# Windowed attention with a gated MLP: all loads through one GpSimd queue, 64-column transposes, and a new list of steps

## The chip, the cores and the metric

One Trainium2 chip, one core. The metric is the device time of one execution in microseconds (us), as a median over several runs. Lower is better. The engines are named as in the profile: PE (TensorE, matrix multiplications), PEld (its weight loads), DVE (VectorE), ACT (ScalarE), POOL (GpSimd) and SP (SyncE, which here only issues transfers).

## What is computed

Four batches, eight heads, 768 positions, head size 64. First an attention with a sliding window of 128 and four sink positions that every query sees, then a block with a gated MLP whose gate mixes along the sequence:

```python
scores = scale * np.matmul(q, k.transpose(0, 1, 3, 2))
keep = (pos[None, :] < 4) | ((rel >= 0) & (rel < 128))        # rel = query position - key position
a = softmax(np.where(keep, scores, -1e9))
x = np.matmul(a, v)                                           # heads side by side: [4, 768, 512]
h = gelu_tanh(x @ w_in)                                       # [4, 768, 1024]
u, v = h[..., :512], h[..., 512:]
v_n = (v - mean(v)) / np.sqrt(var(v) + 1e-6) * g_ln
v_s = np.einsum('ts,bsd->btd', w_sg, v_n) + b_sg[None, :, None]
out = x + (u * v_s) @ w_out
```

All inputs and the output are float32; the kernel multiplies in bf16.

## The kernel before

Everything that the kernel does is cut into small steps, each a function of a few instructions. The string STEPS (lines 15 to 64) lists some 700 of them, and the loop at line 500 issues them in that order. Each engine executes its own instructions strictly in that order, so the list alone decides which work stands ahead of which; a step whose input is late holds up all later steps of its engine. Numbers behind a name are the batch, then the pair of heads (four pairs a batch), then a part. HOLDS (line 68) adds two orders by hand: the loads LQ.1.0 and LG wait until the transfer LWS has landed.

The steps, in the order in which a batch passes through them:

- LQ, LK, LV (lines 171 to 179) load q, k and v of one pair of heads as float32 through SP's queue. q and k come with six consecutive positions of a head in each partition, v with single positions of 64 values. LW, LWS and LWO (lines 196 to 205) load the three weight matrices through GpSimd's queue, which turns float32 into bf16 on the way. LC (line 207) fetches the v of the sink positions through ACT's queue.
- CQ, CK, CV (lines 185 to 194) cast them to bf16, all on GpSimd (line 182).
- TQ, TK (lines 269 to 272, helper at 261) transpose a pair on PE: six transposes of 128 columns, where the two heads of the pair stand side by side. EQ (line 274, DVE) and EK (line 279, ACT) copy the result out of PSUM.
- QK (line 303) multiplies, with one head in the upper and one in the lower 64 rows of the array; EX (line 315, ACT) takes the exponential; MK (line 320) masks, on DVE by a product (line 325) or on GpSimd by two selections (lines 329 and 333). KS, SK, SX (lines 283 to 301) do the same for the sink positions. Batch 0 does this for each pair, the later batches once for all four pairs. SK of a later batch is four products of 512 columns that are added up in one tile.
- AV (line 340) multiplies by v, NR (line 365, DVE) divides by the sums.
- XT, XE (batch 0, PE and ACT) or XD (a transposing transfer) turn the result. MV and MU (lines 394 and 442) multiply by w_in, GV and GU (ACT) apply the gelu.
- BN (line 406, DVE) takes mean and variance, RS (line 414, GpSimd) the inverse root, Z (line 430, DVE or ACT) normalizes. WT and WE turn w_sg once.
- SP (line 463, PE) mixes along the sequence, GT (line 470, DVE) adds the bias, GM (line 475, DVE) multiplies by u, OU (line 479, PE) multiplies by w_out, RA (line 486, DVE) adds x, ST (line 489) stores.

The attention of batch b+1 is mixed with the MLP of batch b. Tiles are handed out from rings (line 110); the two rings in PSUM have 2 and 4 tiles.

Of the kernel before, what the change touches and what calls it, by code (L numbers as in the profile page):

```python
# [15 lines left out]
IDEN ZERO LC MASK LQ.0.0 LK.0.0 LQ.0.1 LK.0.1 VSK LQ.0.2 LK.0.2 LV.0.0 LQ.0.3 LK.0.3 CQ.0.0 LV.0.1 LV.0.2 TQ.0.0  # L16
CK.0.0 VSM.1 LV.0.3 EQ.0.0 TK.0.0 CQ.0.1 EK.0.0 VSM.3 TQ.0.1 CK.0.1 VSM.0 QK.0.0.2 QK.0.0.1 EX.0.0.2 KS.0.0 TK.0.1
EQ.0.1 CQ.0.2 SK.0.0 VSM.2 TQ.0.2 CK.0.2 EQ.0.2 SX.0.0 QK.0.0.0 MK.0.0.2 TK.0.2 EX.0.0.1 CV.0.0 EK.0.2 MK.0.0.1
EX.0.0.0 QK.0.2.2 KS.0.2 CQ.0.3 EX.0.2.2 MK.0.0.0 QK.0.2.0 LW.0 EK.0.1 QK.0.2.1 LW.1 EX.0.2.1 AV.0.0.0 KS.0.1 TQ.0.3
# [4 lines left out]
AV.0.3.0 NR.0.3.0 XT.0.3 XE.0.3 MV.0.2 MU.0.3 GV.0.2 LQ.1.0 LK.1.0 WT.3 WT.4 LV.1.0 WE.3 WT.5 LG WT.2 WE.4 GU.0.3
MV.0.0 WE.5 LQ.1.1 WE.2 LK.1.1 BN.0.2 LV.1.1 MV.0.1 GV.0.0 LQ.1.2 CQ.1.0 LK.1.2 RS.0.2 LV.1.2 BN.0.0 MU.0.0 LQ.1.3
GV.0.1 CK.1.0 LK.1.3 LV.1.3 Z.0.5 WT.1 RS.0.0 LQ.2.0 GU.0.0 TK.1.0 BN.0.1 LK.2.0 MU.0.1 EK.1.0 CV.1.0 Z.0.0 WE.1
TQ.1.0 WT.0 RS.0.1 Z.0.4 Z.0.1 LV.2.0 MU.0.2 WE.0 GU.0.1 EQ.1.0 CQ.1.1 GU.0.2 CK.1.1 Z.0.2 TQ.1.1 LQ.2.1 QK.1.0.2
# [510 lines left out]
```

The softmax here doesn't subtract the row's maximum and nothing guards it: scores larger than these inputs give would overflow.

## Time and profile before

| | |
|---|---|
| median of 11 runs | 172.43 us (171.75 to 173.75) |
| profiled execution | 171.8 us |
| its span in the trace | 169.8 us |
| PE busy in the span | 148.7 us (88%) |
| DVE busy | 139.4 us (82%) |
| ACT busy | 101.8 us (60%) |
| POOL busy | 95.8 us (56%) |
| read from HBM, written to it | 24.81 MB, 6.29 MB |

The span is the time from the first to the last instruction in the trace; some 2 us of the profiled execution lie around it. A row of the profile gives a line of the code, an engine, an operation, the tiles that it writes and reads, how often it occurs, its busy time and the mean of one. [...]

### The profile page before, as it was taken

How to read it: one execution, taken by the hardware profiler on the slowest of the kernel's cores; microseconds unless marked ns; L12 is line 12 of the kernel's file. 1: busy time of each engine (PE TensorE's matmuls, PEld its weight loads, DVE VectorE, ACT ScalarE, POOL GpSimd, SP SyncE). 2: the span in 40 equal slices, each digit the busy share in tenths (PEclk: the TensorE clock that was granted, in tenths of full speed). 3: DMA queues.
4: the chain of work that ended last, by engine and by line, in shares of the span. 5: the costliest groups of instructions: out<-in, count | busy, mean ns of one | idle time of the engine just before them, and what ended most of it. 6: DMA issues, size and time to landing. Idle time of an engine off the chain costs nothing.

```text
span 169.8 us, 3610 instructions
## 1 busy us (share of the span) xinstructions
PE 148.7 (88%) x1375; PEld 89.0 (52%) x1388; DVE 139.4 (82%) x290; ACT 101.8 (60%) x119; POOL 95.8 (56%) x158
## 2 busy tenths in 40 slices
PE   0547888699898999799999999999999999999970
PEld 0323566365555476546576566544665744565530
DVE  6297698449989999999998899838899985959961
ACT  0417889656986859767559985854898006850000
POOL 7779865015999999999598587134306300510000
PEclk9999999999999999999999999999999999999999
DMA  5999989997999999979999102970100474110144
GB/s 163 349 316 234 211 113 190 218 261 238 317 303 300 299 297 296 334 150 248 326 313 290 24 0 41 214 243 0 62 4 0 77 177 180 64 62 0 40 151 185
DMA packets 49617, 30.94 MB, mean 182 GB/s; under 512 B 35904, under 2 KB 46400, under 8 KB 49600
## 3 DMA queue, kind: packets, MB, share of 16 engines
q1 hardware_dynamic: 47072, 27.93, 61.8%
q0 software_dynamic: 2368, 2.75, 10.0%
q8 instruction: 11, 0.18, 0.4%
q14 instruction: 6, 0.05, 0.1%
q10 hardware_dynamic: 160, 0.03, 0.1%
HBM read 24.81 MB, written 6.29 MB: 183 GB/s over the span
## 4 chain that ended last, share of the span: by engine, by line
PE 62%; DVE 20%; ACT 5%; POOL 3%; issue 3%; DMA 3%; ACTq 2%; DVEq 0%
PE mm L466 15%; PE mm L483 11%; PE sc L446 10%; PE sc L399 10%; PE sc L310 5%; PE mm L266 3%; DVE x_sb L370 3%; DVE qT L276 3%; DVE gtmp L471 3%; ACT P L318 3%; PE mm L350 3%; DMA vs<-in_v_dram 3%; DVE P L325 3%; DVE wsg_gated L476 2%; PE mm L356 2%
## 5 line engine op out<-in xcount | busy, mean ns | idle before, releaser
L318 ACT ACTIVATE P<-sc 128x1024 bf16<-128x1024 f32 (+1 forms) x48 | 43.8, 956 | 11.0 <-PE sc L310 9.5
L466 PE MATMUL mm<-wsgT,z 128*128 128x384 bf16 x192 | 34.0, 326 | 0.0
L329 POOL TENSOR_SCALAR_AFFINE_SELECT P<-P 128x512 bf16<-128x512 bf16 x28 | 20.2, 723 | 17.6 <-ACT P L318 13.4
L466 PEld LDWEIGHTS <-z 128*128 128x128 bf16 x192 | 18.0, 98 | 12.1 <-issue 1.2
L483 PE MATMUL mm<-w_out_sb,wsg_gated 128*128 128x512 bf16 x88 | 22.3, 379 | 1.5 <-DVE wsg_gated L476 1.1
L399 PE MATMUL sc<-w_in_sb,xT 128*128 128x512 bf16 x93 | 22.2, 379 | 0.4 <-ACT xT L384 0.2
L446 PE MATMUL sc<-xT,w_in_sb 128*128 128x384 bf16 x128 | 22.4, 326 | 0.0
L471 DVE SCALAR_TENSOR_TENSOR gtmp<-mm,g_sb,b_bc 128x384 bf16<-128x384 f32 x32 | 19.3, 611 | 3.5 <-PE mm L466 3.5
L487 DVE TENSOR_TENSOR ot<-mm,x_sb 128x512 f32<-128x512 f32 x24 | 16.1, 683 | 5.4 <-PE mm L483 5.3
L310 PE MATMUL sc<-qT,kT 64*128 64x256 bf16 x192 | 16.8, 285 | 4.0 <-DVE qT L276 1.6
L182 POOL TENSOR_SCALAR q<-q 128x768 bf16<-128x768 f32 x16 | 14.4, 900 | 9.4 <-DMA q<-in_q_dram 9.4
L404 ACT ACTIVATE vt<-sc 128x1024 f32<-128x1024 f32 x12 | 12.3, 1024 | 11.7 <-PE sc L399 11.7
L350 PE MATMUL mm<-v_sb,P 128*128 128x65 bf16 x192 | 17.3, 197 | 1.8 <-DVE P L325 1.6
L370 DVE TENSOR_TENSOR x_sb<-mm,rcp 128x384 bf16<-128x384 f32 x32 | 17.8, 557 | 1.1
L411 DVE BATCH_NORM_STATS2 st<-vt 128x6 f32<-128x512 f32 x24 | 16.2, 676 | 2.5 <-ACT vt L404 2.5
L350 PEld LDWEIGHTS <-P 128*128 128x128 bf16 x192 | 14.7, 100 | 6.1 <-DVE P L325 2.1
L325 DVE TENSOR_TENSOR P<-P,mask 128x1024 bf16<-128x1024 bf16 x20 | 16.5, 831 | 1.4 <-ACT P L318 1.3
L446 PEld LDWEIGHTS <-w_in_sb 128*128 128x128 bf16 x128 | 12.4, 98 | 8.4
L356 PE MATMUL mm<-v_sb,P 128*128 128x65 bf16 x160 | 16.3, 197 | 0.0
L281 ACT COPY kT<-mm 128x768 bf16<-128x768 bf16 x16 | 12.8, 801 | 5.7 <-PE mm L266 5.7
L182 POOL TENSOR_SCALAR v_sb<-v 128x768 bf16<-128x768 f32 x16 | 14.9, 940 | 1.7 <-DMA v<-in_v_dram 1.5
L476 DVE TENSOR_TENSOR wsg_gated<-gtmp,uT 128x384 bf16<-128x384 bf16 x32 | 15.2, 486 | 0.8
(61 smaller groups left out, 239.1 us busy)
## 6 DMA issues: line engine op xcount, KB each, us to landing
q<-in_q_dram SPq DMA_DIRECT2D x16, 384.0 KB, 6.4
k<-in_k_dram SPq DMA_DIRECT2D x16, 384.0 KB, 5.6
v<-in_v_dram SPq DMA_DIRECT2D x16, 384.0 KB, 6.8
out_dram<-ot SPq DMA_DIRECT2D x24, 256.0 KB, 2.1
wsg_gated<-in_moe_w_sg_dram POOLq DMA_DIRECT2D x1, 1152.0 KB, 9.2
w_in_sb<-in_moe_w_in_dram POOLq DMA_DIRECT2D x2, 512.0 KB, 7.1
w_out_sb<-in_moe_w_out_dram POOLq DMA_DIRECT2D x1, 512.0 KB, 8.4
b_bc<-in_moe_b_sg_dram SPq DMA_DIRECT2D x1, 384.0 KB
```

What stands on the lines that cost most here:

```text
L182: return nc.gpsimd.tensor_scalar(out=dst, in0=src, scalar1=1.0, scalar2=1.0, op0=ALU.mult, op1=ALU.mult)
L310: nc.tensor.matmul(sc[:, hl, 256 * jl:256 * jl + n], kT[b, p][rows, 128 * j:128 * (j + 1)], qT[b, p][rows, 128 * j:128 * j + n], start=Tru ...
L318: nc.scalar.activation(out=pt[:, :, 0:w], in_=sc_ring[b, p, g][:, :, 0:w], func=AF.Exp, scale=scale)
L325: nc.vector.tensor_mul(pt[:, :, 0:w], pt[:, :, 0:w], m.unsqueeze(1).to_broadcast([128, 2, w]))
L329: nc.gpsimd.affine_select(out=p4[:, :, :, 0:128], in_=p4[:, :, :, 0:128], compare_op=ALU.is_ge, fill=0.0, base=0, pattern=[[0, 2], [0, 2], ...
L350: nc.tensor.matmul(av[:, il, hl, :], P[b, p, i // 2][:, hl, 256 * (i % 2):256 * (i % 2) + 128], vb[:, h, i, :], start=first, stop=False)
L370: nc.vector.tensor_mul(xs[:, 3 * half:3 * half + 3, 128 * p:128 * (p + 1)].rearrange("p t (h d) -> p t h d", h=2), av[:, :, :, 0:Dh], rcp. ...
L399: nc.tensor.matmul(hp[:, jl, :], xT[b][:, j, c, :], w_in_sb[:, c, d_half:2 * d_half], start=(c == 0), stop=(c == KD - 1))
L446: nc.tensor.matmul(hp[:, hf, 0:NH], w_in_sb[:, c, 128 * dc:128 * (dc + 1)], xT[b][:, 3 * hf:3 * hf + 3, c, :], start=(c == 0), stop=(c == ...
L466: nc.tensor.matmul(ps[:, 0:NH], z[b][:, si, 128 * dc:128 * (dc + 1)], wsgT[:, si, NH * hf:NH * (hf + 1)], start=(si == 0), stop=(si == NT ...
L471: nc.vector.scalar_tensor_tensor(out=gtmp.new((b, hf, dc)), in0=mm_ring["g", b, hf, dc][:, 0:NH], scalar=g_sb[:, dc:dc + 1], in1=b_bc[:, N ...
L483: nc.tensor.matmul(ps, gatedT[:, (2 * b + hf) % 3, dc, 128 * tl:128 * (tl + 1)], w_out_sb[:, dc, :], start=(dc == 0), stop=(dc == KU - 1))
```

## The change

The loads of q and k, but for the first pair, go through GpSimd's queue and are turned to bf16 on the way (helper `load`); in batch 0 a load brings a pair of heads, later two pairs. v goes through the same queue as float32. The first pair of q and k comes through SP's queue into two tiles of v's ring, and DVE casts it (CQ.0.0 and CK.0.0); no other cast of q and k remains. In GpSimd's queue the first v stands behind q and k of pairs 0, 1 and 2. The hold of LQ.1.0 is gone. LC goes to SP.

The new tiles of q and k hold each head's positions together, and so a transpose now takes 64 columns of one head and writes one half of the partitions: twelve transposes for a pair instead of six. SK of a later batch writes its four products to four groups of 32 partitions, each with 32 columns of weights; the sink tiles get the layout that goes with it.

Steps that can run on several engines get a letter in the list: A is ACT, D is DVE, P is GpSimd. EQ and EK are split between ACT and DVE (EQ 11 and 5, EK 10 and 6; before 16 on DVE and 16 on ACT), CV is split three ways (3 ACT, 5 DVE, 8 GpSimd; before all 16 on GpSimd), MK has 29 on DVE and 19 on GpSimd (before 20 and 28), GM 14 on DVE and 18 on GpSimd (before all 32 on DVE), and two of the four XE are on DVE. The statistics of four rows of tiles are taken together: GpSimd only takes the power, the rest of RS goes to DVE (the end of BN, and NM). DVE fills the constant tiles (FILL, MASK0). `DT` is empty, so the branches that ask for it are not taken.

The list of steps is another one throughout; its first lines, up to the statistics of batch 0, are shown.

```diff
-IDEN ZERO LC MASK LQ.0.0 LK.0.0 LQ.0.1 LK.0.1 VSK LQ.0.2 LK.0.2 LV.0.0 LQ.0.3 LK.0.3 CQ.0.0 LV.0.1 LV.0.2 TQ.0.0
-CK.0.0 VSM.1 LV.0.3 EQ.0.0 TK.0.0 CQ.0.1 EK.0.0 VSM.3 TQ.0.1 CK.0.1 VSM.0 QK.0.0.2 QK.0.0.1 EX.0.0.2 KS.0.0 TK.0.1
-EQ.0.1 CQ.0.2 SK.0.0 VSM.2 TQ.0.2 CK.0.2 EQ.0.2 SX.0.0 QK.0.0.0 MK.0.0.2 TK.0.2 EX.0.0.1 CV.0.0 EK.0.2 MK.0.0.1
-EX.0.0.0 QK.0.2.2 KS.0.2 CQ.0.3 EX.0.2.2 MK.0.0.0 QK.0.2.0 LW.0 EK.0.1 QK.0.2.1 LW.1 EX.0.2.1 AV.0.0.0 KS.0.1 TQ.0.3
-NR.0.0.0 EX.0.2.0 SK.0.1 MK.0.2.2 SK.0.2 MK.0.2.1 AV.0.0.1 SX.0.2 CK.0.3 MK.0.2.0 QK.0.1.0 SX.0.1 QK.0.1.1 CV.0.1
-EX.0.1.0 NR.0.0.1 EQ.0.3 CV.0.2 EX.0.1.1 QK.0.1.2 CV.0.3 MK.0.1.0 TK.0.3 EX.0.1.2 XT.0.0 MK.0.1.1 LWS AV.0.2.1 EK.0.3
-AV.0.2.0 XE.0.0 NR.0.2.1 MK.0.1.2 QK.0.3.2 QK.0.3.1 AV.0.1.0 EX.0.3.2 KS.0.3 NR.0.2.0 SK.0.3 LWO AV.0.1.1 EX.0.3.1
-NR.0.1.0 QK.0.3.0 MK.0.3.2 XT.0.2 SX.0.3 NR.0.1.1 EX.0.3.0 MK.0.3.1 XT.0.1 XE.0.2 AV.0.3.1 MK.0.3.0 XE.0.1 NR.0.3.1
-AV.0.3.0 NR.0.3.0 XT.0.3 XE.0.3 MV.0.2 MU.0.3 GV.0.2 LQ.1.0 LK.1.0 WT.3 WT.4 LV.1.0 WE.3 WT.5 LG WT.2 WE.4 GU.0.3
-MV.0.0 WE.5 LQ.1.1 WE.2 LK.1.1 BN.0.2 LV.1.1 MV.0.1 GV.0.0 LQ.1.2 CQ.1.0 LK.1.2 RS.0.2 LV.1.2 BN.0.0 MU.0.0 LQ.1.3
-GV.0.1 CK.1.0 LK.1.3 LV.1.3 Z.0.5 WT.1 RS.0.0 LQ.2.0 GU.0.0 TK.1.0 BN.0.1 LK.2.0 MU.0.1 EK.1.0 CV.1.0 Z.0.0 WE.1
...
+ZERO IDEN LQ.0.0 LK.0.0 LQ.0.1 FILL LK.0.1 LC VSK MASK LQ.0.2 MASK0 CQ.0.0.D LK.0.2 TQ.0.0 LV.0.0 EQ.0.0.D TQ.0.1
+LQ.0.3 CK.0.0.D EQ.0.1.A TK.0.0 LK.0.3 EK.0.0.A VSM.0 LV.0.1 TK.0.1 VSM.1 EK.0.1.A QK.0.0.2 QK.0.0.1 TQ.0.2 KS.0.0
+LV.0.2 EX.0.0.2 VSM.3 SK.0.0 EQ.0.2.D TK.0.2 LV.0.3 EK.0.2.D EX.0.0.1 QK.0.0.0 MK.0.0.2.D LW.0 SX.0.0 KS.0.1 QK.0.2.1
+MK.0.0.1.D SK.0.1 EX.0.0.0 LW.1 TQ.0.3 CV.0.0.D KS.0.2 EX.0.2.1 AV.0.0.1 LWS MK.0.0.0 TK.0.3 VSM.2 SX.0.1 QK.0.1.1 LWO
+EQ.0.3.A QK.0.2.2 EK.0.3.D SK.0.2 EX.0.2.2 LQ.1.0 AV.0.0.0 MK.0.2.1.D SX.0.2 LK.1.0 KS.0.3 MK.0.2.2.D EX.0.1.1 LV.1.0
+NR.0.0.1 CV.0.2.A QK.0.3.1 MK.0.1.1.D QK.0.2.0 SK.0.3 EX.0.3.1 CV.0.1.P NR.0.0.0 AV.0.2.1 CV.0.3.P EX.0.2.0 XT.0.0
+NR.0.2.1 QK.0.1.0 XE.0.0.D MK.0.3.1.P EX.0.1.0 QK.0.1.2 EX.0.1.2 MK.0.2.0 LV.1.1 QK.0.3.2 MK.0.1.0 EX.0.3.2 AV.0.2.0
+QK.0.3.0 LQ.1.1 MK.0.1.2.D SX.0.3 NR.0.2.0 EX.0.3.0 MK.0.3.2.P AV.0.1.0 AV.0.1.1 NR.0.1.0 LK.1.1 XT.0.2 AV.0.3.1
+MK.0.3.0 XE.0.2.A LV.1.2 NR.0.1.1 AV.0.3.0 NR.0.3.1 XT.0.1 LV.1.3 NR.0.3.0 XE.0.1.A LQ.2.0 XT.0.3 XE.0.3.D LK.2.0
+MV.0.2 LG WT.2 GV.0.2 WT.5 WE.2 WT.4 MV.0.1 WE.5 WE.4 BN.0.2 MV.0.0 GV.0.1 MU.0.0 RS.0.2 GV.0.0 NM.0.2 Z.0.4.A WT.0
+BN.0.0 TQ.1.1 GU.0.0 TQ.1.0 MU.0.2 EQ.1.1.A BN.0.1 Z.0.5.A TK.1.0 GU.0.2 MU.0.1 EK.1.0.A EQ.1.0.D RS.0.1 MU.0.3 WE.0
+GU.0.1 CV.1.0.D NM.0.1 LV.2.0 TK.1.1 Z.0.1.D Z.0.0.A QK.1.0.0 CV.1.1.D WT.1 GU.0.3 EK.1.1.D WT.3 LV.2.1 EX.1.0.0
...
-HOLDS = "LQ.1.0<LWS LG<LWS"
+HOLDS = "LG<LWS"
+
+
+DT = ()
...
-    q32 = Ring("q32", 4, [128, 2, NT * Dh], F32)
-    k32 = Ring("k32", 4, [128, 2, NT * Dh], F32)
+    q32 = Ring("q32", 2, [128, 2, NT, Dh], F32)
+    k32 = Ring("k32", 2, [128, 2, NT, Dh], F32)
+    qn = Ring("qn", 2, [128, NT, 2, Dh], BF16)
+    kn = Ring("kn", 2, [128, NT, 2, Dh], BF16)
     v32 = Ring("v32", 4, [128, 2, NT, Dh], F32)
-    q16 = Ring("q16", 3, [128, NT, 2, Dh], BF16)
-    k16 = Ring("k16", 3, [128, NT, 2, Dh], BF16)
+    q16 = Ring("q16", 3, [128, 4, NT, Dh], BF16)
+    k16 = Ring("k16", 3, [128, 4, NT, Dh], BF16)
...
-    ks_w = NS // HP
+    ks_w = 128 // HP
...
+    def load(ring, src, b, i):
+        n = 2 if b == 0 else 4
+        hs = slice(n * i, n * i + n)
+        dst = ring.get((b, n * i // 4))[:, n * i % 4:n * i % 4 + n].rearrange("p h t d -> p h (t d)")
+        return nc.gpsimd.dma_start(out=dst, in_=src[b, hs].rearrange("h (p t) d -> p h (t d)", p=128))
+
+    def rows(eng, ring, src, b, p):
+        return eng.dma_start(out=ring.new((b, p)).rearrange("p h t d -> p (h t) d"),
+                                 in_=src[b, 2 * p:2 * p + 2].rearrange("h (t p) d -> p (h t) d", p=128))
+
+    def first(name, src):
+        return nc.sync.dma_start(out=v32.new(name).rearrange("p h t d -> p h (t d)"),
+                                 in_=src[0, 0:2].rearrange("h (p t) d -> p h (t d)", p=128))
+
+    def LQ(b, i):
+        if (b, i) == (0, 0):
+            return first("q", q)
+        return rows(nc.sync, q32, q, b, i) if b in DT else load(q16, q, b, i)
+
+    def LK(b, i):
+        if (b, i) == (0, 0):
+            return first("k", k)
+        return rows(nc.sync, k32, k, b, i) if b in DT else load(k16, k, b, i)
 
     def LV(b, p):
-        return nc.sync.dma_start(out=v32.new((b, p)).rearrange("p h t d -> p (h t) d"),
-                                 in_=v[b, 2 * p:2 * p + 2].rearrange("h (t p) d -> p (h t) d", p=128))
-
-    def cast(dst, src):
+        return rows(nc.sync if b in DT else nc.gpsimd, v32, v, b, p)
+
+    def copy(e, dst, src):
+        if e == "A":
+            return nc.scalar.copy(dst, src)
+        if e == "D":
+            return nc.vector.tensor_copy(dst, src)
         return nc.gpsimd.tensor_scalar(out=dst, in0=src, scalar1=1.0, scalar2=1.0,
                                        op0=ALU.mult, op1=ALU.mult)
 
-    def CQ(b, p):
-        return cast(q16.new((b, p)).rearrange("p t h d -> p h t d"),
-                    q32[b, p].rearrange("p h (t d) -> p h t d", d=Dh))
-
-    def CK(b, p):
-        return cast(k16.new((b, p)).rearrange("p t h d -> p h t d"),
-                    k32[b, p].rearrange("p h (t d) -> p h t d", d=Dh))
-
-    def CV(b, p):
-        return cast(v_sb[b % 2][:, 2 * p:2 * p + 2, :, 0:Dh], v32[b, p])
+    def CQ(b, p, e):
+        if b == 0:
+            return copy(e, q16.get((0, 0))[:, 0:2], v32["q"])
+        return copy(e, qn.new((b, p)).rearrange("p t h d -> p h t d"), q32[b, p])
+
+    def CK(b, p, e):
+        if b == 0:
+            return copy(e, k16.get((0, 0))[:, 0:2], v32["k"])
+        return copy(e, kn.new((b, p)).rearrange("p t h d -> p h t d"), k32[b, p])
+
+    def CV(b, p, e):
+        return copy(e, v_sb[b % 2][:, 2 * p:2 * p + 2, :, 0:Dh], v32[b, p])
 
...
-        for s in range(n_sink):
-            nc.scalar.dma_start(out=vs32[s:NS:n_sink, :, :], in_=v[:, :, s, :].rearrange("b h d -> h b d"))
+        for i in range(n_sink):
+            nc.sync.dma_start(out=vs32[i:128:16, :, :], in_=v[:, :, i, :].rearrange("b h d -> h b d"))
...
     def transposes(name, ring, b, p):
-        src = ring[b, p].rearrange("p t h d -> p t (h d)")
+        src = ring[b, p // 2]
         mm_ring.new((name, b, p))
         ps = psb((name, b, p))
         for t in range(NT):
-            nc.tensor.transpose(ps[:, t, :], src[:, t, :], iden)
+            for hl in range(2):
+                nc.tensor.transpose(ps[64 * hl:64 * hl + 64, t, :], src[:, 2 * (p % 2) + hl, t, :], iden)
...
     def SK(b, p0):
-        prs = range(HP) if b else (p0,)
         ps = mm_ring.new(("s", b, p0))
-        for n, p in enumerate(prs):
-            nc.tensor.matmul(ps, ks_sink[b % 2][:, 128 * p:128 * (p + 1)], qT[b, p][:, 256:768],
-                             start=(n == 0), stop=(n == len(prs) - 1))
+        ks = ks_sink[b % 2]
+        if b == 0:
+            nc.tensor.matmul(ps, ks[:, 128 * p0:128 * (p0 + 1)], qT[b, p0][:, 256:768], start=True, stop=True)
+            return
+        for p in range(HP):
+            c0 = (128 + ks_w) * p
+            nc.tensor.matmul(ps[ks_w * p:ks_w * (p + 1), :], ks[:, c0:c0 + ks_w], qT[b, p][:, 256:768],
+                             start=True, stop=True)
...
+        if jj:
+            nc.vector.tensor_scalar(out=rs.get(b)[:, part(jj)], in0=mv[:, part(jj), 1], scalar1=1e-6,
+                                    scalar2=None, op0=ALU.add)
 
     def RS(b, jj):
-        mv = stats[b, jj]
-        rs = tiny.tile([128, 2], F32, name="rs")
-        stats[b, jj] = (mv, rs, None)
-        nc.gpsimd.tensor_scalar(out=rs, in0=mv[:, :, 1], scalar1=1e-6, scalar2=1.0,
-                                op0=ALU.add, op1=ALU.mult)
-        nc.gpsimd.tensor_tensor(rs, rs, neg_half, op=ALU.pow)
-        if 2 * jj >= ZACT:
-            return
-        nmr = tiny.tile([128, 2], F32, name="nmr")
-        nc.gpsimd.tensor_tensor(nmr, rs, mv[:, :, 0], op=ALU.mult)
-        nc.gpsimd.tensor_scalar(out=nmr, in0=nmr, scalar1=-1.0, scalar2=1.0, op0=ALU.mult, op1=ALU.mult)
-        stats[b, jj] = (mv, rs, nmr)
-
-    ZACT = 2
-
-    def Z(b, j):
-        jj, jl = j // 2, j % 2
-        mv, rs, nmr = stats[b, jj]
-        zt = z.get(b)
-        if j < ZACT:
-            nc.scalar.activation(out=zt[:, j, :], in_=vt[b, jj][:, jl, :], func=AF.Identity,
-                                 bias=nmr[:, jl:jl + 1], scale=rs[:, jl:jl + 1])
+        r = rs[b][:, part(jj)]
+        nc.gpsimd.tensor_tensor(r, r, neg_half[:, part(jj)], op=ALU.pow)
+
+    def NM(b, jj):
+        nc.vector.scalar_tensor_tensor(out=nmr.get(b)[:, part(jj)], in0=mvs[b][:, part(jj), 0], scalar=-1.0,
+                                       in1=rs[b][:, part(jj)], op0=ALU.mult, op1=ALU.mult)
+
...
-    def GM(b, hf, dc):
-        nc.vector.tensor_mul(gatedT[:, (2 * b + hf) % 3, dc, :], gtmp[b, hf, dc],
+    def GM(b, hf, dc, e):
+        (nc.vector if e == "D" else nc.gpsimd).tensor_mul(gatedT[:, (2 * b + hf) % 3, dc, :], gtmp[b, hf, dc],
                              uT[b][:, dc, NH * hf:NH * (hf + 1)])
```

## The prediction

> **What bounds the kernel now.** I read the page's busy times first, then the chain of work that ended last, then the busy times by stage.
>
> ```profile
> PE 148.7 (88%) x1375; PEld 89.0 (52%) x1388; DVE 139.4 (82%) x290; ACT 101.8 (60%) x119; POOL 95.8 (56%) x158
> ...
> PE 62%; DVE 20%; ACT 5%; POOL 3%; issue 3%; DMA 3%; ACTq 2%; DVEq 0%
> ```
>
> PE has most of the chain. By stage (length, then busy PE, PEld, DVE, ACT, POOL):
>
> ```profile
> 0.00:33.10 33.10, 19.80 (x229) 13.23 (x231) 23.95 (x48) 19.82 (x26) 22.60 (x42) 1.00 1.05 223
> 33.10:78.10 45.00, 42.63 (x451) 26.47 (x457) 40.72 (x80) 34.00 (x40) 38.06 (x55) 1.00 1.08 277
> 78.10:111.00 32.90, 32.72 (x325) 19.87 (x325) 30.18 (x67) 24.16 (x29) 23.21 (x37) 1.00 0.72 182
> 111.00:138.00 27.00, 26.95 (x238) 15.59 (x237) 23.02 (x54) 14.96 (x17) 8.86 (x18) 1.00 0.22 61
> ```
>
> The first stage, batch 0's attention, ends with the first MV; nothing is full in it, it is a chain of loads, casts, exponentials and masks. From 33 us PE is busy almost throughout. Its real price is the distance between starts, in the timeline of PE (start, duration, engine, line):
>
> ```profile
> 50.52 0.39 PE L310 MATMUL sc<-qT,kT 64*128 64x256 bf16 x4
> 50.84 1.15 PE L466 MATMUL mm<-wsgT,z 128*128 128x384 bf16 x6
> 51.92 0.39 PE L310 MATMUL sc<-qT,kT 64*128 64x256 bf16 x4
> 52.25 1.15 PE L466 MATMUL mm<-wsgT,z 128*128 128x384 bf16 x6
> 53.23 0.50 PE L266 MATMUL mm<-iden,q 128*128 128x128 bf16 x6
> 53.57 0.50 PE L266 MATMUL mm<-iden,k 128*128 128x128 bf16 x6
> ```
>
> Six transposes take 53.57 − 53.23 = 0.34 us, 0.056 each. Six products of SP take 0.98 ahead of transposes (52.25 to 53.23) but 1.08 ahead of QK (50.84 to 51.92): going over to 64 rows costs 0.1 us. Four products of QK, 256 columns each, take 0.32 with such a change, so 0.22 without: 0.055 each, half of what 256 columns cost at SP's rate (384 columns in 0.163). Two 64-row products run beside each other.
>
> I priced each step of the old list so (0.217 for 512 columns, 0.163 for 384, 0.056 for 128, 0.030 for AV's 65, whose starts at 102.71 and 102.74 are that far apart), with 0.1 for each change of shape: 13.8 us of PE work before the first MV and 127.0 after it. The first MV starts at some 32.5, the last product near 165.7: 133 us for 127 of work, so PE idles only some 6 us after stage one.
>
> [...]
>
> **The change part by part.**
> *Transposes (PE).* Twelve for six; 24 of the 32 steps lie after stage one; the other eight lie in it, where PE has 13.8 us of work in 33 and hides them (uncovered, 8 × 0.16 = 1.3). Low bound: the two halves run beside each other like QK's rows: 0.34 a step, no loss. Next: each takes a full slot[...]: 0.67.[...] I take 0.50, midway between the first two, since the rows speak for overlap[...]: 24 × (0.50 − 0.34) = +3.9 (0 to +8.0[...]).
> *Changes of shape.* Transposes now have a shape of their own. Counted in both lists: 46 changes after stage one before, 71 now; 25 × 0.1 = +2.5.
> *SK.* Three batches with four products of 0.217; in four column groups beside each other I take 0.31 (0.22 to 0.87): 3 × (0.87 − 0.31) = −1.7. AV, MV, SP and the rest are unchanged.
> PE after stage one: +4.7, in a stage where it has no cover.
> *GpSimd.* Gone: 32 casts of q and k (14.4 + 13.7 = 28.1), 8 of v (7.5), 9 masks (4 × 1.37 + 5 × 1.19 = 11.4), RS but for eight powers (7.8), constants (2). Added: 34 issues of loads at the 0.87 of the w_sg row (29.6; v has more and shorter runs, so up to 1.5 each, +10 more)[...]. Sum −12: 84 of 170 us. It was full from 46 to 73 us (26.6 busy of 26.8), and its order held a cast of q for 0.5 us of PE's time at 46.2.
> *DVE.* EQ −11 × 0.945 = −10.4; EK +6 × 0.945 = +5.7 (same shape); MK +9 × 0.75 = +6.8; GM −18 × 0.486 = −8.7; seven casts at 0.7 (0.45 to 0.95): +4.9; two XE at 0.55: +1.1; small statistics, 16 × 0.18 = +3.0; constants −0.5. Sum +1.9, hidden behind PE after stage one; without that cover it would cost its 1.9.
> *ACT.* EQ +11 × 0.80, EK −6 × 0.80, CV +3 × 0.80, XE −2 × 0.86: +4.7, to 106 of 170, hidden behind PE (34 of 45 us busy in the fullest stage; uncovered, 4.7).
> *SP's queue.* 48 loads leave it and four small ones (LC) come. ST and XD no longer stand behind loads there; but what they wait for longest is DVE's result (35.0 and 31.2 us in the list of waits), so nothing is gained or lost. LC lands later than now (SP issues it third), ahead of the first VSM near 8.4 us; VSM no longer stands ahead of EQ.0.0 on DVE, where it held the first QK until 10.2.
> *Idle time given back.* In the last stage, PE waits 1.1 us for the last GM (163.1). The new list puts the last SP ahead of the other half's OU, which covers that. With the 0.5 above: about −1.5 of the 6.
> *Stage one.* The first pair still comes through SP and is cast: q by DVE while it idles, then EQ.0.0, and only then k, so QK starts near 10.3 as now (10.2). From there ACT has some 18 us of its own, DVE some 22: constants 3.5, VSM 5.5, EQ and EK 3.8, MK 7.5, NR 6, other 2.9, together 29 for the stage, against 24 now. 0.9 + 29 = 30 is DVE's floor; with half of the nine us that it idles now, 34.5: +1.0 to +1.5. I take +1.0 (−3 to +4).
> *Waits added.* In the built program GpSimd's loads take eight semaphores in turn, so an issue waits for the load eight before it, and all of GpSimd's later work behind it. RS.0.2 now stands behind LK.2.0, which waits for LK.1.0. Up to its end 11.8 MB must come (twelve first loads of 0.39, weights 5.5 as float32, two of 0.79). The old order had some 9.2 MB by 32 us, 305 GB/s from 2 us on: 11.8 / 0.305 + 2 = 40.7 us, against 39.8, when RS.0.2 runs now. Nearly met, and PE has MV, MU and WT to do meanwhile: 0, or the 0.9 if that work were done. At 250 GB/s it is not met (a rival below).
>
> **Sum.** +4.7 − 1.5 + 1.0 = +4.2. On the profiled execution (171.8 for a span of 169.8): 176.0. The median of the runs shown lies 0.6 above that one, so 176.6, rounded to 176.5.
>
> **The rivals.**
> *Full overlap of the column halves, nothing else moves.* 0.34 a step: PE +0.9, with the other terms +0.4: 172.8. For it: QK's rows.[...]
> *Faster: stage one shrinks.* q and k come as bf16 and pass no cast on GpSimd, which fed PE there (the trace has 5.6 us of PE waiting for the first cast of q). At DVE's floor the first MV comes at 30, −3.1. With 0.34 a step: 0.9 − 1.5 − 3.1 = −3.7, a median of 168.7. It decides if the first MV starts before 31.5 and a transposing step takes at most 0.40. Against it: DVE gets five us more work there.
> *The queue.* If one GpSimd queue brings 250 GB/s, LK.1.0 ends at 11.8 / 0.25 + 2 = 49.2 instead of 40.7. RS.0.2, Z and all SP of batch 0 wait, and so do batch 1's transposes: up to +8.5 on the forecast, 185. For it: v comes in 256-byte runs[...]. Against it: the weights went through this queue at a good rate. Serial transposes at 0.67 alone give +4: 180.6.
> *Not what it says.* The built order has one GpSimd queue for all loads but the first pair, the sinks and the biases, so that it happens is not in doubt.
>
> **Chances.** Forecast, with 174 to 182 as its own range: 0.45. Full overlap alone (171.5 to 174): 0.15. Stage one shorter (below 171.5): 0.22. Queue or a slower transpose (above 182): 0.18. The range of 168 to 188 leaves out the ends of the last two. A change of less than 0.5% (171.6 to 173.3) can't be told from none. Faster 0.21 (most of the third case), same 0.08, slower 0.71.
>
> **What would show it.** Right: a transposing step takes near 0.5 from start to start in PE's timeline, the first MV starts at 33 to 34, SK of a later batch takes 0.3, GpSimd is near 84 us. Wrong: steps at 0.34 or above 0.7; PE waiting for GpSimd's power or for a load around 40 to 56 us; the first MV before 31.5; issues of v far above 0.9 us.

## The result, and the profile after

Median 177.74 us after (12 runs, 174.69 to 181.76), 172.67 before (47 runs, 171.11 to 173.84). The ratio of the times near each kernel's fastest is 1.0198, with a 95% interval of 1.016 to 1.0236; it leaves out the seven slowest of the twelve runs after, and as these come at least in part from the change itself (experiment 2), the medians of all runs stand beside the ratios below. The change is slower by 3.4 to 5.1 us. The profiled execution took 174.69 us for a span of 173.0, the fastest of the twelve.

The page of the changed kernel, busy times and then the chain that ended last:

```profile
PE 147.4 (85%) x1569; PEld 87.0 (50%) x1580; DVE 136.0 (79%) x306; ACT 105.5 (61%) x125; POOL 91.2 (53%) x120
...
PE 51%; DMA 27%; DVE 8%; ACT 7%; issue 3%; POOL 2%; DVEq 0%; POOLq 0%; ACTq 0%
DMA k<-in_k_dram 16%; PE mm L488 15%; PE mm L505 9%; PE sc L468 9%; PE sc L428 8%; DMA xT<-x_sb 6%; DMA v<-in_v_dram 5%; ACT P L352 4%; PE sc L344 3%; PE mm L294 2%; PE mm L384 2%; DVE gtmp L493 1%; DVE st L441 1%; PE mm L390 1%; DVE x_sb L404 1%
```

PE has 194 products more and is no busier. Transfers have gone from 3% of the chain to 27%, and one of them, `xT<-x_sb` (XD, the transposing transfer that SP issues), appears in the prediction only under SP's queue, where it was to lose nothing. By stage (length, then busy PE, PEld, DVE, ACT, POOL):

```profile
0.00:29.80 29.80, 16.41 (x276) 11.71 (x278) 23.53 (x59) 19.53 (x25) 23.91 (x36) 1.00 1.08 200
29.80:78.10 48.30, 43.42 (x560) 26.06 (x561) 39.69 (x85) 35.92 (x45) 34.42 (x43) 1.00 0.98 194
78.10:111.00 32.90, 30.61 (x332) 18.27 (x333) 25.71 (x58) 22.44 (x27) 16.32 (x22) 1.00 0.55 116
```

Stage one ends with the first MV. In PE's timeline, before and then after:

```profile
32.08 0.81 PE L399 MATMUL sc<-w_in_sb,xT 128*128 128x512 bf16 x2
```

```profile
29.77 2.14 PE L428 MATMUL sc<-w_in_sb,xT 128*128 128x512 bf16 x7
```

It starts 2.3 us earlier (the 33.1 shown before lies a little behind the first MV). The next two stages give it back: PE idles 4.9 of 48.3 us (before 2.4 of 45.0), and 2.3 of 32.9 (before 0.2). The list of PE's waits says for whom (us in total, times, longest):

```profile
PE sc L468 <- ACT uT L473: 2.8, 2, 2.2
PE sc L428 <- DMA xT<-x_sb: 2.2, 1, 2.2
```

The first is batch 0's MU, whose buffer comes free late because ACT and DVE stand behind a power on GpSimd. That power in GpSimd's timeline (start, duration, operation, and in brackets the idle time before it):

```profile
37.47 0.76 POOL L182 DMA_DIRECT2D q<-in_q_dram  x1 [1.69 <-DMA q<-in_q_dram]
39.50 0.75 POOL L182 DMA_DIRECT2D k<-in_k_dram  x1 [1.27 <-DMA k<-in_k_dram]
40.26 0.74 POOL L449 TENSOR_TENSOR rs<-rs,neg_half 128x2 f32<-128x2 f32 x1
```

and in DVE's:

```profile
35.41 0.33 DVE L444 TENSOR_SCALAR rs<-mvs 128x2 f32<-128x2 f32 x1
41.04 0.16 DVE L452 SCALAR_TENSOR_TENSOR nmr<-mvs,rs 128x2 f32<-128x2 f32 x1 [5.29 <-POOL rs L449]
```

The power's input is ready at 35.74; it starts at 40.26, since two issues of loads (LQ.2.0, LK.2.0) stand ahead of it and each waits for an earlier load. DVE does nothing for 5.29 us.

The second wait is the transposing transfer of batch 1's second half, XD.1.1. SP's timeline, and then GpSimd's for the same time:

```profile
71.16 1.55 SPq L419 DMA_TRANSPOSE xT<-x_sb  x1
72.82 1.27 SPq L512 DMA_DIRECT2D out_dram<-ot  x2
74.19 3.17 SPq L419 DMA_TRANSPOSE xT<-x_sb  x1
77.45 9.84 SPq L512 DMA_DIRECT2D out_dram<-ot  x4
```

```profile
73.30 2.13 POOL L185 DMA_DIRECT2D v<-in_v_dram  x2
75.40 0.79 POOL L182 DMA_DIRECT2D q<-in_q_dram  x1
76.15 0.80 POOL L182 DMA_DIRECT2D k<-in_k_dram  x1
76.88 2.12 POOL L185 DMA_DIRECT2D v<-in_v_dram  x2
```

Batch 3's loads go out on GpSimd's queue from 73.30 on, just ahead of SP's transfer at 74.19. In the chain that transfer takes 10.73 us; the others for which the trace has a landing take 3.6 to 3.8. PE gets its columns at 84.96:

```profile
84.96 2.76 PE L428 MATMUL sc<-w_in_sb,xT 128*128 128x512 bf16 x12 [2.16 <-DMA xT<-x_sb]
```

In the kernel before, the loads of this data stood behind both transfers in SP's own queue, the first of them at 77.89, and the transfers landed in 3.7 to 4.6 us:

```profile
70.09 1.67 SPq L388 DMA_TRANSPOSE xT<-x_sb  x1
...
74.92 1.44 SPq L388 DMA_TRANSPOSE xT<-x_sb  x1
76.45 1.33 SPq L490 DMA_DIRECT2D out_dram<-ot  x2
77.89 0.40 SPq L178 DMA_DIRECT2D v<-in_v_dram  x1
```

In the changed kernel one store is held too: DVE waits 3.5 us for `out_dram<-ot` at 86.23.

### The profile page after: what moved, and what is told of

Read it like the earlier page. It is cut to its first block, busy times and chain, and to the rows that moved or that the text cites. A ratio compares the mean times of both kernels' runs of the same rounds, so it can differ in the third digit from the quotient of the medians.

```text
span 173.0 us, 3927 instructions
## 1 busy us (share of the span) xinstructions
PE 147.4 (85%) x1569; PEld 87.0 (50%) x1580; DVE 136.0 (79%) x306; ACT 105.5 (61%) x125; POOL 91.2 (53%) x120
## 4 chain that ended last, share of the span: by engine, by line
PE 51%; DMA 27%; DVE 8%; ACT 7%; issue 3%; POOL 2%; DVEq 0%; POOLq 0%; ACTq 0%
DMA k<-in_k_dram 16%; PE mm L488 15%; PE mm L505 9%; PE sc L468 9%; PE sc L428 8%; DMA xT<-x_sb 6%; DMA v<-in_v_dram 5%; ACT P L352 4%; PE sc L344 3%; PE mm L294 2%; PE mm L384 2%; DVE gtmp L493 1%; DVE st L441 1%; PE mm L390 1%; DVE x_sb L404 1%
## 5 line engine op out<-in xcount | busy, mean ns | idle before, releaser
L488 PE MATMUL mm<-wsgT,z 128*128 128x384 bf16 x192 | 35.1, 327 | 0.2 <-ACT qT L207 0.2
L498 POOL TENSOR_TENSOR wsg_gated<-gtmp,uT 128x384 bf16<-128x384 bf16 x18 | 17.5, 982 | 16.8 <-DVE gtmp L493 16.7
L488 PEld LDWEIGHTS <-z 128*128 128x128 bf16 x192 | 17.5, 98 | 12.9 <-issue 2.3
L359 DVE TENSOR_TENSOR P<-P,mask 128x1024 bf16<-128x1024 bf16 (+1 forms) x29 | 22.3, 778 | 1.1 <-ACT P L352 0.8
L505 PE MATMUL mm<-w_out_sb,wsg_gated 128*128 128x512 bf16 x89 | 22.3, 379 | 0.6 <-DVE x_sb L404 0.2
L185 POOL DMA_DIRECT2D v<-in_v_dram x16 | 17.2, 1084 | 8.2 <-DMA wsg_gated<-in_moe_w_sg_dram 4.2
L363 POOL TENSOR_SCALAR_AFFINE_SELECT P<-P 128x512 bf16<-128x512 bf16 x19 | 14.5, 762 | 12.0 <-ACT P L352 12.0
L344 PE MATMUL sc<-qT,kT 64*128 64x256 bf16 x192 | 15.7, 269 | 4.9 <-ACT P L352 3.6
L432 ACT ACTIVATE vt<-sc 128x1024 f32<-128x1024 f32 x12 | 12.3, 1024 | 12.0 <-PE sc L428 12.0
L449 POOL TENSOR_TENSOR rs<-rs,neg_half 128x2 f32<-128x2 f32 (+1 forms) x8 | 6.9, 865 | 24.0 <-DVE rs L444 22.4
L384 PE MATMUL mm<-v_sb,P 128*128 128x65 bf16 x192 | 16.5, 194 | 2.2 <-POOL P L363 1.1
L468 PEld LDWEIGHTS <-w_in_sb 128*128 128x128 bf16 x128 | 12.3, 98 | 11.8 <-issue 3.0
L428 PEld LDWEIGHTS <-xT 128*128 128x128 bf16 x96 | 9.1, 98 | 13.3 <-DMA xT<-x_sb 2.7
L390 PE MATMUL mm<-v_sb,P 128*128 128x65 bf16 x160 | 15.6, 194 | 0.0
## 6 DMA issues: line engine op xcount, KB each, us to landing
wsg_gated<-in_moe_w_sg_dram POOLq DMA_DIRECT2D x1, 1152.0 KB, 18.2
```

Source lines behind the costliest of these rows:

```text
L344: nc.tensor.matmul(sc[:, hl, 256 * jl:256 * jl + n], kT[b, p][rows, 128 * j:128 * (j + 1)], qT[b, p][rows, 128 * j:128 * j + n], start=Tru ...
L359: nc.vector.tensor_mul(pt[:, :, 0:w], pt[:, :, 0:w], m.unsqueeze(1).to_broadcast([128, 2, w]))
L384: nc.tensor.matmul(av[:, il, hl, :], P[b, p, i // 2][:, hl, 256 * (i % 2):256 * (i % 2) + 128], vb[:, h, i, :], start=first, stop=False)
L428: nc.tensor.matmul(hp[:, jl, :], xT[b][:, j, c, :], w_in_sb[:, c, d_half:2 * d_half], start=(c == 0), stop=(c == KD - 1))
L468: nc.tensor.matmul(hp[:, hf, 0:NH], w_in_sb[:, c, 128 * dc:128 * (dc + 1)], xT[b][:, 3 * hf:3 * hf + 3, c, :], start=(c == 0), stop=(c == ...
L488: nc.tensor.matmul(ps[:, 0:NH], z[b][:, si, 128 * dc:128 * (dc + 1)], wsgT[:, si, NH * hf:NH * (hf + 1)], start=(si == 0), stop=(si == NT ...
```

## The experiments

"The jam" below is the late XD.1.1, "the power" the wait of 5.3 us for it.

**1. The power's wait removed.** The two issues go behind batch 0's powers:

```diff
-XE.0.1.A LQ.2.0 XT.0.3 XE.0.3.D LK.2.0
+XE.0.1.A XT.0.3 XE.0.3.D
...
-EQ.1.0.D RS.0.1 MU.0.3
+EQ.1.0.D RS.0.1 LQ.2.0 LK.2.0 MU.0.3
```

> The changed kernel with one move: the loads LQ.2.0 and LK.2.0 stand behind RS.0.1 in GpSimd's order instead of ahead of RS.0.2. Theory Q (GpSimd's powers of batch 0 stand behind an issue that waits for a load, and DVE, ACT and PE wait behind them): the 5.3 us wait of DVE for the power goes, the median falls from 177.7 by 2 to 4 us, to about 174.5. Rival P (the loss is PE's own work: 64-column transposes and changes of shape): same as the changed kernel, 177 to 178.5.

Measured: 177.88 us (175.09 to 181.57), ratio 1.0214 (1.0157 to 1.027): nothing gained. GpSimd now idles 1.5 us until the power's input is there, so that wait is gone, but in this profile (an execution of 178.65 us; the other was of 174.69) the jam is longer:

```profile
87.59 4.45 PE L428 MATMUL sc<-w_in_sb,xT 128*128 128x512 bf16 x12 [4.64 <-DMA xT<-x_sb]
```

The wait is 4.64 us instead of 2.16, and the twelve products behind it take 4.45 us instead of 2.76: PE ran at some 0.6 of its pace, and the mean granted clock of this execution is 0.99 against 0.998. The two differences, 2.5 and 1.7, are about the distance of the two executions, 178.65 − 174.69 = 4.0. Up to the wait they are level: it begins at 82.95 here and at 82.76 there, though the first MV starts 1.8 us later here (31.54). So by then this execution had won back what it lost in stage one, which fits the power's move, and the jam took it again. Whether the longer jam comes from the move or from the spread of the runs, one profile of each kernel doesn't tell.

**2. The jam removed.** Batch 3's loads wait until XD.1.1 has landed:

```diff
-HOLDS = "LG<LWS"
+HOLDS = "LG<LWS LV.3.0<XD.1.1"
```

> The changed kernel with one more hold: LV.3.0 waits until XD.1.1 has landed, so that batch 3's six loads can't stand ahead of it in the DMA engines. Theory D (the second half of batch 1's transposing transfer, which takes over 10 us, stops PE before MV.1.1): XD.1.1 lands within 4 to 5 us, PE's wait of 2.2 us for it goes, the median falls by 1.5 to 3 us, to about 175.5. Rival P: 177 to 178.5. A rival of D: the loads then come too late for batch 3 and the wait returns at CV.3.0, 177 to 179.

Measured: 173.34 us (171.97 to 175.02, 22 runs), ratio 1.0031 (1.0009 to 1.0052): 4.4 us less by medians, 2.9 by the ratios (1.5 to 3 were expected), and the spread falls from 7 us to 3. GpSimd's and then PE's timeline of this kernel:

```profile
78.05 2.12 POOL L185 DMA_DIRECT2D v<-in_v_dram  x2 [5.79 <-DMA xT<-x_sb]
```

```profile
76.42 1.89 PE L428 MATMUL sc<-w_in_sb,xT 128*128 128x512 bf16 x8
80.77 3.62 PE L428 MATMUL sc<-w_in_sb,xT 128*128 128x512 bf16 x15
```

GpSimd idles until XD.1.1 has landed, 4.9 us after its start at 73.20; that idle time costs nothing, and PE runs its products without the wait. The harm came from the loads that start beside the transfer.

**3. Both.**

> Both moves together. Theory Q and D: the two gains add, 171 to 173 us, about level with the kernel before. Rival P: above 176.

Measured: 172.55 us (171.49 to 174.65, 14 runs), ratio 0.9968 (0.9937 to 0.9999). The interval lies wholly below that of experiment 2: with the jam gone, the power is worth some 0.6%, 0.8 us by medians. It is less than the wait; one reason is that DVE has a new stop. DVE's timeline, then GpSimd's:

```profile
54.97 0.61 DVE L493 SCALAR_TENSOR_TENSOR gtmp<-mm,g_sb,b_bc 128x384 bf16<-128x384 f32 x1
55.50 3.50 DVE L498 TENSOR_TENSOR wsg_gated<-gtmp,uT 128x384 bf16<-128x384 bf16 x1
59.10 0.62 DVE L493 SCALAR_TENSOR_TENSOR gtmp<-mm,g_sb,b_bc 128x384 bf16<-128x384 f32 x1
```

```profile
55.03 0.95 POOL L498 TENSOR_TENSOR wsg_gated<-gtmp,uT 128x384 bf16<-128x384 bf16 x1
55.90 0.67 POOL L363 TENSOR_SCALAR_AFFINE_SELECT P<-P 128x512 bf16<-128x512 bf16 x1
56.49 0.45 POOL L367 TENSOR_SCALAR_AFFINE_SELECT P<-P 128x256 bf16<-128x256 bf16 x1
56.87 0.66 POOL L363 TENSOR_SCALAR_AFFINE_SELECT P<-P 128x512 bf16<-128x512 bf16 x1
57.46 0.43 POOL L367 TENSOR_SCALAR_AFFINE_SELECT P<-P 128x256 bf16<-128x256 bf16 x1
57.85 0.92 POOL L498 TENSOR_TENSOR wsg_gated<-gtmp,uT 128x384 bf16<-128x384 bf16 x1
```

A gate product whose median is 0.36 us takes 3.50, from 55.50 to 59.00; GpSimd works from 55.03 to 58.77 without a gap.

**4. The halves alone.** The kernel before, with each transpose of q and k in two products of 64 columns and nothing else changed:

```diff
-            nc.tensor.transpose(ps[:, t, :], src[:, t, :], iden)
+            for hl in range(2):
+                nc.tensor.transpose(ps[64 * hl:64 * hl + 64, t, :], src[:, t, 64 * hl:64 * hl + 64], iden)
```

> The kernel before with one part of the change alone: each transpose of q and k in two halves of 64 columns, twelve for a pair instead of six, everything else as before. Step at 0.34 to 0.37 us as the trace of the changed kernel shows it, plus 0.1 us for each further change of shape that falls into PE-bound stretches: +1 to +3, 174 to 175.5 us. The forecast's 0.50 a step: +5 to +6, 178. If neither costs anything: 172.7.

Measured: 175.06 us (174.31 to 176.0), ratio 1.0147 (1.0114 to 1.0181): +2.2 us by medians, +2.5 by the ratio. PE's timeline:

```profile
56.44 0.53 PE L267 MATMUL mm<-iden,q 128*64 128x128 bf16 x12
56.80 0.50 PE L267 MATMUL mm<-iden,k 128*64 128x128 bf16 x12
57.20 0.53 PE L267 MATMUL mm<-iden,q 128*64 128x128 bf16 x12
```

Twelve half transposes take 0.36 and 0.40 from start to start, where six whole ones took 0.34 (the products' records overlap in the trace: in the kernel before, one of 512 columns lasts 0.379 us, and sixteen start 0.216 apart). The halves themselves cost 24 × 0.02 to 0.06, 0.5 to 1.4 us after stage one. The rest can be the changes of shape around them, but this isn't shown: in this execution (176.0 us, the slowest of the six) the first MV starts at 34.82, 2.7 us later than before, and the span from there on is 1.8 us longer (174.3 − 34.82 against 169.8 − 32.08). Only these 1.8 us hold the halves and shapes after stage one. What whole transposes would give in the changed kernel has not been measured.

**5. The slow product moved.** Experiment 3 with that one gate product on GpSimd:

```diff
-GM.0.0.0.D
+GM.0.0.0.P
```

> Both moves of before (e3), and GM.0.0.0 on GpSimd instead of DVE. In e3's profile this product, 0.36 us elsewhere, lasted 3.50 us, as long as GpSimd ran five instructions without a pause, and ended with them. Theory S [...]: DVE is free for the next GT some 3 us earlier, the median falls by 1 to 3 us from 172.5, to 170 to 171.5. Rival (DVE waited for an operand, or DVE isn't what limits there): unchanged, 172 to 173, or later by GpSimd's 0.9 us.

Measured: 171.73 us (171.12 to 174.03, 15 runs), ratio 0.9943 (0.9912 to 0.9973). No gate product of DVE takes over 1.06 us now. Experiments 3 and 5 stood on different chips, so both were repeated side by side.

> The version with batch 3's loads held and the two loads behind the power (172.55 us beside a kernel before of 172.83), once more, on the same chip and in the same rounds as the next kernel, since the two were timed on different chips. Theory: DVE's gate product is starved while GpSimd works without a gap, 3.5 us instead of 0.36, and this is on the way to the end; 0.5 to 1.2 us slower than the next kernel, and the 3.5 us product is in the profile again. Rival: the stalled product is covered; the two kernels agree within 0.4 us.

> The same with the one gate product GM.0.0.0 on GpSimd instead of DVE (171.73 us beside a kernel before of 172.89). Theory: no product of DVE takes over 1.1 us, and the time is 0.5 to 1.2 us below the last kernel's, some 0.6% below the kernel before. Rival: within 0.4 us of the last kernel.

Measured: 172.67 us (171.3 to 174.4, 22 runs), ratio 0.9966 (0.9939 to 0.9993), with the product on DVE; 171.67 us (170.46 to 173.06, 6 runs), ratio 0.9885 (0.9821 to 0.995), with it on GpSimd. The gate products on DVE, first in the repeat of experiment 3, then in that of 5 (duration in ns: least, median, most):

```profile
L498 DVE TENSOR_TENSOR wsg_gated<-gtmp,uT x14: 348/358/3496, 51.4 to 161.2; 128x384 bf16<-128x384 bf16 x14
```

```profile
L498 DVE TENSOR_TENSOR wsg_gated<-gtmp,uT x13: 349/358/1060, 54.1 to 161.7; 128x384 bf16<-128x384 bf16 x13
```

The slow product comes back (3.495 us, then 3.496), and moving it gave 0.8 us once and 1.0 the other time; the repeats taken together, 172.66 us (36 runs) against 171.73 (21). The two intervals of each pair still touch, so this is a likely size and not a proven one. The kernel with all three edits is the fastest of the study, 1.2 to 1.35 us below the kernel before.

**6. v on SP's queue.** The changed kernel, with v's 16 loads on SP and q and k on GpSimd:

```diff
-        return rows(nc.sync if b in DT else nc.gpsimd, v32, v, b, p)
+        return rows(nc.sync, v32, v, b, p)
```

> The changed kernel with v through SP's queue again, so two queues instead of one. In SP's order LV.3.0 stands behind XD.1.1. Theory D (what hurts is that batch 3's loads overtake XD.1.1): four of the six loads now come behind it, XD.1.1 lands some 2 to 3 us sooner, the median falls by 1.5 to 4 us from 177.7, to 174 to 176, and GpSimd issues 17 us less. Rival (the cost is the single queue's rate or its issue time on GpSimd): below 172. Rival (SP's queue holds v up behind stores and LG): above 178.

Measured: 190.53 us (189.19 to 192.41), ratio 1.1012 (1.0953 to 1.1072), far from what the theory expected. The rival that had it above 178 put this down to stores and LG in front of v; but in SP's queue the first eight v follow one another from 5.05 us on, and LG comes at 41.69. PE's timeline and then the DMA queues from 6 to 36 us (packets, MB, share of time):

```profile
37.18 0.21 PE L384 MATMUL mm<-v_sb,P 128*128 128x65 bf16 x1 [15.18 <-ACT v_sb L207]
```

```profile
q0 software_dynamic: 4647, 4.42, 89.2%
q1 hardware_dynamic: 5398, 1.36, 31.2%
```

The first v's are cast at 15.09, 26.40 and 36.30: one load of 0.39 MB in some 10 or 11 us, 35 to 40 GB/s of the 190 to 200 that the core moves. In the two lines the packets are shared 5398 to 4647, but SP's carry 252 bytes on the mean (1.36 MB / 5398) and GpSimd's 951, so v gets a quarter of the bytes (1.36 of 5.78 MB) while loads that are needed later pass it. PE then idles 15.18 us, and its granted clock is 0.50 from 26 to 36 us. One queue for q, k and v keeps the order of need; the kernel before has that on SP's queue, and the change keeps it on GpSimd's.

**7. Stage one's sharing-out undone.** Experiment 3 with batch 0's casts, evacuations and masks on the engines that had them before (EQ on DVE, EK.0.2 and EK.0.3 on ACT, CV.0.0 and CV.0.2 on GpSimd, XE.0.0 and XE.0.3 on ACT, three masks on GpSimd and one on DVE).

> Both moves (e3), and in batch 0 the old assignment: EQ on DVE, EK, XE on ACT, CV on GpSimd, the third mask group on GpSimd. Theory L (the first MV starts at 29.6 instead of 32.1 because q and k need no cast on GpSimd): first MV within 1 us of 29.6, median 172 to 173.5. Rival W (it starts earlier because the work of the first stage is shared out between the engines): first MV at 31.5 to 33, median 174 to 176.

Measured: 174.73 us (174.43 to 175.93), ratio 1.013 (1.0079 to 1.0182), 2.1 to 2.2 us above experiment 3 and its repeat by medians, 2.8 by the ratios. So the sharing-out is worth between 2 and 3 us. That it is so by the start of the first MV is not shown: it starts at 32.3 here and at 29.6 in experiment 3 and its repeat, but at 32.3 and 32.7 in experiment 5 and its repeat too, where batch 0 has the same list as in 3. Over the first 30 us the granted clock is 0.83 in experiment 7's profile and 0.96 in that of 5's repeat, and 1.00 in those of 3 and its repeat.

**8. The first v earlier, and later.** Experiment 3 with LV.0.0 behind two pairs of q and k instead of three, as the diff shows, and, in another kernel, behind all four:

```diff
-MASK LQ.0.2 MASK0 CQ.0.0.D LK.0.2 TQ.0.0 LV.0.0 EQ.0.0.D
+MASK LV.0.0 LQ.0.2 MASK0 CQ.0.0.D LK.0.2 TQ.0.0 EQ.0.0.D
```

> Both moves (e3), with the first v behind two pairs of q and k in the queue instead of three. q and k of pair 2 then come some 1.2 us later, CV.0.0 has its v earlier, which it needs only at 14 us. If the place of the first v matters: pair 2's transposes at 10.6 us wait, first MV 0.5 to 1.2 us later, median 173 to 173.7. If it doesn't: 172.5.

> The version with both loads moves (172.55 us) with the first v behind all four pairs of q and k instead of three. With v behind two pairs it took 176.07. If the place of v trades q and k against v and three pairs is the balance, the first AV now waits for v, the other way round: 173.5 to 176. If q and k are all that counts, 171 to 172.5. The place of the first AV's wait in PE's list shows which.

Measured: two pairs 176.07 us (175.14 to 178.06), ratio 1.0178 (1.0128 to 1.0229); four pairs 173.84 (171.88 to 176.25, 19 runs), ratio 1.0007 (0.9973 to 1.0041); three pairs 172.55. Earlier costs 3.5 us, more than the 0.5 to 1.2 expected. In its profile (178.06 us, the slowest of the six) PE waits 2.2 us for a q at 13.06 and the first MV starts at 35.6, with the granted clock at 0.89 over the first 30 us and 0.90 over the next 20; how much of the 3.5 is the wait and how much the clock is open. Later costs 0.4% by the ratios, whose intervals overlap, and not as expected: AV waits 0.2 us for v in its profile, no more than in experiment 3's. The third pair is needed ahead of v; whether the fourth is, this doesn't settle.

**9. PE kept busy in the jam.** The changed kernel, with twelve more products in front of the one that waits for XD.1.1, written to the place that it overwrites (L429 in the lines below; the true product is L432 there):

```diff
+            if (b, j) == (1, 3):
+                for c in 3 * list(range(KD)):
+                    nc.tensor.matmul(hp[:, jl, :], xT[b][:, j - 1, c, :], w_in_sb[:, c, d_half:2 * d_half],
+                                     start=(c == 0), stop=(c == KD - 1))
```

> The changed kernel with twelve more products of 512 columns (2.6 us of PE's work at 0.216 each; their result is overwritten) in front of the first product that waits for the held-up transposing transfer of batch 1. The profiles put PE's wait there at 2.2 us in the run of 174.7 us and at 4.6 us in the first experiment's run of 178.7 us, where twelve products after it took 4.45 us instead of 2.76: TensorE's clock was down. Clock theory: part of what the queue's jam costs is not the wait but the lower clock after a wait [...]; with the wait cut to 2 us the mean granted clock of the runs rises from some 0.98 to above 0.99 and the median falls by 1 to 2.5 us, to 175.2 to 176.7, though work is added. Rival, the wait alone: the filler lies in the wait, where it is free when the transfer is late and costs up to 2.6 when it is not; the median stays at 177.7 or rises to 178.5.

Measured: 176.67 us (175.78 to 178.95), ratio 1.0234 (1.0165 to 1.0302). The median of the runs' mean granted clocks is 0.994, against 0.980 for the changed kernel, whose runs go from 174.69 us at 0.998 to 178.91 at 0.980 and 181.76 at 0.964. PE's timeline:

```profile
81.77 2.75 PE L429 MATMUL sc<-w_in_sb,xT 128*128 128x512 bf16 x12
85.87 2.76 PE L432 MATMUL sc<-w_in_sb,xT 128*128 128x512 bf16 x12 [1.34 <-DMA xT<-x_sb]
```

The transfer was as late as ever (4.1 us of filler and wait), and the products after it run at full speed, 2.76 for twelve. So PE kept its pace after this wait of 1.34 us. After the one of 4.64 us in experiment 1 it didn't (4.45 for twelve), nor after the one of 15.18 us in experiment 6, where the granted clock is 0.59 from 30 to 50 us. The length of a wait is not all: in experiment 7's profile AV's products start 0.055 us apart from 26.2 to 29.1 us, against 0.030 at 22.3, and the clock over the first 30 us is 0.83, with no wait of PE over 1.5 us after its first products. The clock of the runs rose as the theory had it. The time doesn't prove it: the median fell by 1.1 us with 2.6 us of work added, but the ratio rose, and the intervals overlap. So a wait that costs twice, once by itself and once by the clock after it, is a possible reason why the changed kernel's runs lie so far apart, and not a shown one: here a run at 0.997 still took 178.13 us, and in experiment 2 one at 0.964 took 173.48. A run's mean clock doesn't say in which stage it was down.

## Why the prediction came out, point by point

177.74 was measured and 176.5 forecast. The total was right by luck: errors of several us cancel. Of its signs of being right only SK's 0.3 came; of its signs of being wrong two did, the first MV before 31.5 and PE's wait behind the power (to 42.85).

- **Transposes, +3.9: wrong size.** "I take 0.50, midway between the first two" failed; it was the author's estimate. A step takes 0.36 to 0.40, close to the low bound: column halves run beside each other like rows, at 0.060 to 0.067 us for two, where a whole transpose takes 0.056. In the changed kernel 24 of them (first row below) take 38.73 − 37.93 = 0.80, with the change to MU's shape. So +0.5 to +1.4.
- **Changes of shape, +2.5: probably too high.** Experiment 4 has +2.2 to +2.5 for halves and shape together, and in its profile 1.8 after stage one. With 0.5 to 1.4 for the halves, 0.4 to 2.0 are left. This term has not been measured alone.
- **SK, −1.7: right.** Four products in column groups, with the change after them, take 59.11 − 58.78 = 0.33 (0.31 forecast); 3 × (0.87 − 0.33) = −1.6.

```profile
37.93 0.86 PE L294 MATMUL mm<-iden,q 128*64 128x128 bf16 x24
38.73 1.47 PE L468 MATMUL sc<-xT,w_in_sb 128*128 128x384 bf16 x8
...
58.78 0.40 PE L330 MATMUL mm<-qT,ks_sink 128*32 128x512 bf16 x4
59.11 1.15 PE L488 MATMUL mm<-wsgT,z 128*128 128x384 bf16 x6
```

- **Stage one, +1.0: wrong sign.** The first MV starts at 29.77, not 33 to 34, 2.3 us before the old one. The working took DVE's 29 us as a floor with half of its idle time on top; DVE did 23.5 of them by then. Experiment 7 puts the sharing-out at −2 to −3 us in the whole. The 2.3 us of the two profiles are no firm size: experiment 1 has the same list up to there, and its first MV starts 1.8 us later. PE's pace differs, though the recorded clock of stage one is 1.00 in the changed kernel's profile and the mean of experiment 1's execution is 0.99; the first k transposes after 11 us, in the changed kernel and then in experiment 1:

```profile
11.87 0.53 PE L294 MATMUL mm<-iden,k 128*64 128x128 bf16 x12 [0.46 <-issue]
```

```profile
12.55 0.85 PE L294 MATMUL mm<-iden,k 128*64 128x128 bf16 x12 [0.98 <-DVE ks_sink L317]
```

In the kernel before, six whole transposes still take 0.85 us at 19.19, and 0.49 from 23.83 on, with a recorded clock of 1.00 in that whole stage. So part of the 2.3 us can be PE's pace in these executions and not the change.

- **Waits added, 0: a right time, held against a wrong one.** "11.8 / 0.305 + 2 = 40.7 us, against 39.8" gave the power's start to 0.4 us (40.26), and the issues waited as the working has it, each for the load eight before: LV.1.2 4.18 us for LWS, LV.1.3 1.33 for LWO, LQ.2.0 1.69 for LQ.1.0, LK.2.0 1.27 for LK.1.0. (The "good rate" of the weights in GpSimd's queue: in the profile before, w_sg's 1152 KB landed 9.2 us after the issue; in the changed kernel, 18.2.) But 39.8 is when the old kernel wanted it; with a shorter stage one and fewer copies of DVE ahead of the statistics it was wanted at 35.74. The wait of 5.3 us is worth 0.8 us, and only once the jam is gone (experiments 1 and 3).
- **SP's queue, "nothing is gained or lost": the step that failed most.** Loads that leave a queue no longer wait in it. Six loads of batch 3 (3.1 MB as float32), which SP's order had held behind XD, now start beside it, and XD.1.1 takes 10.7 us instead of 4. Experiment 2 prices that at 2.9 to 4.4 us. The queue rival had the right kind of cause, a load in the way, at the wrong place: it looked at one queue's rate up to 40 us, not at two queues side by side at 74.
- **Idle time given back, −1.5: given back in its place, lost elsewhere.** The last GM no longer keeps PE waiting; behind the power and in the jam PE waits 2.8 and 2.2 us.
- **Engines.** GpSimd 91.2 us, not 84: an issue of v takes 1.08 us (0.87 taken; one of q or k takes 0.77) and a gate product 0.98. The 84 was the author's estimate; no trace of the kernel before shows a gate product on GpSimd. DVE's casts of v took 0.62 us (0.7 taken). ACT 105.5 (106 forecast), DVE 136.0 (141). None of them is the bound.

Both signs of the faster rival are there (first MV before 31.5, steps at 0.40 or less), and its 168.7 is 9 us off, in part because it too put SP's queue and the waits at nothing. The parts that stay once the jam, the power and the slow product are mended are +2.2 (halves and shape), −1.6 (SK) and −2.2 (sharing-out), by medians, together −1.6; the mended kernel has −1.2 to −1.35.

## What to carry to other kernels

When transfers move from one queue to another, write down what they stood behind: a FIFO's order is a wait that nobody wrote, and the transfer that it protected is the one to look at. When a step becomes ready earlier, price every wait added against its new time, not the old one. And a long wait of PE can cost more than its own length: after 4.64 us in experiment 1 the next twelve products took 4.45 us instead of 2.76.

## What the runs showed of the hardware that was not expected

- DVE's product of two bfloat16 tiles of 384 columns took 3.50 us instead of 0.36 (experiment 3 and its repeat) while GpSimd worked without a gap, and ended 0.2 us after GpSimd's stretch. In experiment 2 GpSimd has the same stretch and the worst product beside it is one of DVE's masks, 1.80 us instead of 0.68. This points to DVE being held by GpSimd; no run moves GpSimd's work and leaves DVE's, and what else it takes is open.
- Two column halves of 64 of a transpose cost 0.06 to 0.07 us a pair, about what one whole transpose costs (0.056).
- A load in packets of 252 bytes, beside another queue with packets of 951, got 35 to 40 GB/s of some 195.
- The same instructions can run at two paces in stage one: twelve half transposes take 0.53 us from 11.87 on in the changed kernel's profile, and 0.85 us at 12.55 in experiment 1's; in the kernel before, six whole ones take 0.85 us at 19.19 and 0.49 from 23.83 on. What sets the moment is open.
